# A fused attention and maxout kernel: program order from simulated engines, the score bias added on VectorE, one transpose a step, weights scaled in threes

## The chip, the cores and the metric

The kernel runs on one core of one Trainium2 chip. The metric is the device time in microseconds (us), the median of several executions. The engines are named as in the profile: PE multiplies matrices (PEld is its weight load), DVE and ACT work on vectors, POOL is the slower vector engine, and SP here only issues DMAs. Each engine works through its own instructions strictly in the order in which the program put them; semaphores make one wait for another.

## The reference

```python
# q, k, v: (8, 8, 576, 64); s: (8, 8, 576)
scores = (1 / sqrt(64)) * q @ k.T
cum = cumsum(max(s, 0))
bias = -(cum[:, None] - cum[None, :])
scores = where(causal, -1e9, scores + minimum(bias, 0))
scores = scores - max(scores)
attn = exp(scores); attn = attn / (sum(attn) + 1e-9)
x = (attn @ v)                      # heads side by side: (4608, 512)
h = maximum(maximum(x @ w1, x @ w2), x @ w3)      # (4608, 768)
out = h @ w_out                                   # (4608, 512)
```

Attention is causal, with a decay bias from the running sum of `s`; its rows go through three up projections, of which the largest is kept, and one down projection. Weights come as 64-bit floats.

## The kernel before

**Precision.** Every operand of a matmul is split into a high and a low part, and three products (high x high, high x low, low x high) stand for one.

**Attention.** The 64 heads are taken in 32 pairs (8 batches of 4 pairs). A step is one block of 128 queries of a pair against its causal keys: block `qb` 0 to 3 has 128, 256, 384 or 512 keys for both heads, and block 4 (64 queries, 576 keys) puts both heads on the 128 partitions. There are 160 steps. The first 32 are blocks 0 and 1 of batches 0 to 3, the next 48 are blocks 2 to 4 of the same batches, and the other 80 take batches 4 to 7 whole. A step `t` runs so:

- `scores(t)` on PE: the three products and a fourth one for the bias (`kb` against `qr` or `q4`, prepared from the running sum in `cumulate` and `spread`), and the causal mask through `identb` and `tri`, all added up in a PSUM tile `s`, of which there are two (L329, L333, L349, L353).
- `highest(t)` on DVE: the row maximum `nm` (L360). `expo(t)` on ACT: the exponential in place in PSUM with its sum (L370), then `se` (L374).
- `probs(t)`: the reciprocal `ri` on DVE (L394), the high half `prh` on ACT (L410), and the low half `prl` on DVE, which reads `s` in PSUM and `prh` in SBUF (L413). Then SP issues one DMA transpose of `prh` into `ph` and one of `prl` into `pl` (L416, L422), with a third for the tail of block 4.
- `values` after blocks 1 and 4: the product with the split values `vh` and `vl` into `av` (L463), and the evacuation into the expert input `x` by ACT (L473) and DVE (L474).

The splits of q and k (`prep2`, `prep3`) make `qkh` on ACT and `qkl` on POOL for k (L271) and on DVE for q (L274).

**Weights.** 24 tiles of weights (18 up, 6 down) are decoded from 64 bits by one ACT and three DVE instructions (L495 to L504). They are scaled by a power of two, found in `gram1`, `gram2` and `wscale` for six tiles at once, and split on ACT (L573) and DVE (L578).

**Experts.** 256 or 320 tokens of a batch are a set; there are 16. A set has 18 up groups of 12 matmuls (`pm`, three PSUM tiles, L608) and 4 down groups of 18 (`po`, L650). ACT takes the first `pm` of three to `m` (L622), DVE the maximum with the next two (L625); ACT and POOL split the result into `hh` and `hl` (L614, L615); ACT evacuates `po` (L658).

**Order.** The order is written out in one loop over the steps. Hand-written tables (`begun`, `scaled`, `split`) say at which step which weight is loaded, decoded and split, and a counter `cost` lets expert groups in between the scores according to an assumed PE time of a step (`STEP_NS`).

Of the kernel before, what the change touches and what calls it, by code (L numbers as in the profile page):

```python
# [17 lines left out]
PSUM = bass.MemoryType.PSUM  # L18


@with_exitstack
def kernel(
# [16 lines left out]
    K0 = QP  # L39
# [3 lines left out]
    NFT = NW // 4  # L43
    NB = qkv0.shape[0]
# [33 lines left out]
    R = {}

    def scale_of(v):  # L80
        b, _, qbs = visits[v]
        return (b, 0 if qbs[-1] == 1 else 1)

    def load_start(v, dma):
        g = visits[v][1]
        t = wpool.tile([P, N], F32, tag=f"r{RAW - NP + v}", name=f"st{v}")
        dma(out=t, in_=qkv0[0, g, :, 0:512])
        rv = io.tile([P, QKV - V0], F32, tag=f"rv{g}", name=f"rv{v}")[:, 0:256]
        dma(out=rv, in_=qkv0[0, g, :, 512:768])
        rv = rv.rearrange("p (j k d) -> p j k d", j=2, d=D)  # L90
        R[v] = dict(q=t[:, 0:256], k=t[:, 256:512], rv=rv, c=(0, 512), ko=256, qo=0)

    def load(v, dma=None):
        if v < NP:
            return
        b, g, qbs = visits[v]
        t = io.tile([P, V0], F32, tag="raw", name=f"raw{v}", bufs=2)
        if qbs[-1] == 1:
            (dma or nc.sync.dma_start)(out=t[:, 0:512], in_=qkv0[b, g, :, 0:512])
            R.setdefault(v, {}).update(q=t[:, 0:256], k=t[:, 256:512], c=(0, 512), ko=256, qo=0)  # L100
            return
        c0 = 0 if qbs[0] == 0 else 256
        (dma or nc.sync.dma_start)(out=t[:, c0:V0], in_=qkv[b, g, :, c0:V0])
        R.setdefault(v, {}).update(q=t[:, c0:QP], k=t[:, QP:V0], c=(c0, V0), ko=K0, qo=c0)

    def load_v(v, dma=None):
        if v < NP:
            return
        b, g, qbs = visits[v]
        t = io.tile([P, QKV - V0], F32, tag=f"rv{g}", name=f"rv{v}")  # L110
        src = qkv[b, g, :, V0:QKV]
        if qbs[-1] == 1:
            t, src = t[:, 0:256], qkv0[b, g, :, 512:768]
        (dma or nc.sync.dma_start)(out=t, in_=src)
        R.setdefault(v, {})["rv"] = t.rearrange("p (j k d) -> p j k d", j=2, d=D)

    s_t = att.tile([HB, S], F32, tag="qkh", name="s_t")
    nc.sync.dma_start(out=s_t, in_=s)
    load_start(0, nc.scalar.dma_start)
    load_start(1, nc.sync.dma_start)  # L120
    warm = small.tile([P, 1], F32, tag="warm", name="warm", bufs=1)
    nc.vector.memset(warm, 0.0)
    nc.scalar.activation(out=warm, in_=warm, func=AF.Exp)

    raw_w = {}

    def load_w(i, dma=None):
        w = wpool.tile([P, 2 * N], F32, tag=f"r{i % RAW}", name=f"r{i}")
        (dma or nc.sync.dma_start)(out=w.bitcast(I64), in_=wts[i])
        raw_w[i] = w  # L130


    ident = att.tile([P, P], F32, tag="q4", name="ident")
    make_identity(nc, ident)
    identb = const.tile([P, P], BF16, name="identb")
    tri = const.tile([P, P], BF16, name="tri")
    tri4 = const.tile([P, D], BF16, name="tri4")
    nc.gpsimd.memset(tri, 0.0)
    nc.gpsimd.affine_select(
        out=tri, in_=tri, pattern=[[-1, P]], compare_op=ALU.is_ge, fill=NEG, base=0, channel_multiplier=1  # L140
    )
    nc.gpsimd.memset(tri4, 0.0)
    for j in range(2):
        r = slice(j * D, (j + 1) * D)
        nc.gpsimd.affine_select(
            out=tri4[r], in_=tri4[r], pattern=[[-1, D]], compare_op=ALU.is_ge, fill=NEG, base=0, channel_multiplier=1
        )
    nc.vector.tensor_scalar(out=identb, in0=ident, scalar1=1.0 / VSC, scalar2=None, op0=ALU.mult)
    blk = const.tile([P, P], F32, name="blk")
    nc.gpsimd.memset(blk, 0.0)  # L150
    for j in range(2):
        r = slice(j * D, (j + 1) * D)
        nc.gpsimd.memset(blk[r, r], 1.0)
    ones = const.tile([P, 2], F32, name="ones")
    nc.gpsimd.memset(ones, 0.0)
    sel = io.tile([HB, 2, 2, 160], F32R, tag="raw", name="sel", bufs=2)
    nc.gpsimd.memset(sel.bitcast(F32), 0.0)
    for j in range(2):
        nc.gpsimd.memset(ones[64 * j + 32:64 * j + 64, 0:1], 1.0)
        nc.gpsimd.memset(ones[64 * j:64 * j + 32, 1:2], 1.0)  # L160
        for T in range(2):
            a = 32 * j + 16 * T
            for c in range(2):
                o = 32 + 64 * j + 16 * c
                nc.gpsimd.tensor_copy(out=sel[:, T, c, o:o + 16], in_=ident[0:HB, a:a + 16])
    i16 = const.tile([P, 16], F32, name="i16")
    nc.vector.tensor_reduce(out=i16, in_=ident.rearrange("p (a s) -> p s a", s=16), axis=AX.X, op=ALU.add)


    KB, QR = [], []  # L170

    def cumulate():
        r_t = att.tile([HB, S], F32, tag="qkl", name="r_t")
        nc.vector.tensor_scalar(out=r_t, in0=s_t, scalar1=0.0, scalar2=None, op0=ALU.max)
        c_t = att.tile([HB, S], F32, tag="pTh1", name="c_t", bufs=1)
        nc.vector.tensor_tensor_scan(out=c_t, data0=r_t, data1=r_t, initial=0.0, op0=ALU.add, op1=ALU.max)
        cc = att.tile([HB, 2, S], F32R, tag="pTl1", name="cc", bufs=1)
        nc.vector.tensor_copy(out=cc[:, 0], in_=c_t)
        nc.vector.tensor_tensor(out=cc[:, 1], in0=c_t, in1=cc[:, 0].bitcast(F32), op=ALU.subtract)
        cn = const.tile([HB, 2, 6], F32R, name="cn")  # L180
        cf = cc.bitcast(F32)
        for a, c in ((slice(0, 4), slice(64, Q4, P)), (slice(4, 6), slice(Q4 + 32, Q4 + 34))):
            nc.vector.tensor_scalar(out=cn[:, :, a], in0=cf[:, :, c], scalar1=-1.0, scalar2=None, op0=ALU.mult)
        C.update(cc=cc, cn=cn)

    C = {}

    def spread(T):

        cc, cn = C["cc"], C["cn"]  # L190
        ka = ps_m.tile([P, 512], F32, tag="m", name=f"ka{T}")
        kc = ps_m.tile([P, 512], F32, tag="m", name=f"kc{T}")
        for c in range(2):
            nc.tensor.matmul(ka, lhsT=sel[:, T, c, 32:160], rhs=cc[:, c, 0:512], start=(c == 0), stop=(c == 1))
        for c in range(2):
            nc.tensor.matmul(
                kc[:, 0:64], lhsT=sel[:, T, c, 32:160], rhs=cc[:, c, 512:S], start=(c == 0), stop=(c == 1)
            )
        for c in range(2):
            nc.tensor.matmul(  # L200
                kc[:, 64:70], lhsT=sel[:, T, c, 0:128], rhs=cn[:, c, :], start=False, stop=(c == 1),
                skip_group_check=True,
            )
        kb = const.tile([P, S], F32R, name=f"kb{T}")
        nc.scalar.activation(out=kb[:, 0:512], in_=ka, func=AF.Identity, bias=ones[:, 0:1])
        nc.scalar.activation(out=kb[:, 512:S], in_=kc[:, 0:64], func=AF.Identity, bias=ones[:, 0:1])
        KB.append(kb)
        qr = const.tile([P, 16, 5], F32R, name=f"qr{T}")
        nc.vector.scalar_tensor_tensor(
            out=qr, in0=kc[:, 64:69].unsqueeze(1).to_broadcast([P, 16, 5]), scalar=ones[:, 1:2],  # L210
# [234 lines left out]
    def values(v, ph):  # L445
# [22 lines left out]
        def out():  # L468
# [8 lines left out]
            if g == NP - 1:  # L477
                add_set(b, ph)
# [405 lines left out]
```

## Time and profile before

| | |
|---|---|
| time, median of 3 (lowest, highest) | 995.35 us (994.73, 995.59) |
| the profiled execution | span of 993.9 us, 1.4 us below the median of the times |
| PE busy | 879.7 us (89%), 7580 matmuls |
| DVE busy | 574.7 us (58%) |
| ACT busy | 580.5 us (58%) |
| POOL busy | 171.1 us (17%) |
| DMA | 109.51 MB, mean 110 GB/s |

Busy time is the time in which an engine has an instruction in work; a busy PE can still run at a lower granted clock (1.00 is full speed). In a row of a group the line of the code comes first, then the engine, the operation, output and inputs, the shapes, how often, and behind the bars the busy us and mean ns of one, and the idle us of the engine just before with what ended them. In a row of the timeline the first two numbers are the start and the length in us.

### The profile page before, as it was taken

How to read it: one execution, taken by the hardware profiler on the slowest of the kernel's cores; microseconds unless marked ns; L12 is line 12 of the kernel's file. 1: busy time of each engine (PE TensorE's matmuls, PEld its weight loads, DVE VectorE, ACT ScalarE, POOL GpSimd, SP SyncE). 2: the span in 40 equal slices, each digit the busy share in tenths (PEclk: the TensorE clock that was granted, in tenths of full speed). 3: DMA queues.
4: the chain of work that ended last, by engine and by line, in shares of the span. 5: the costliest groups of instructions: out<-in, count | busy, mean ns of one | idle time of the engine just before them, and what ended most of it. 6: DMA issues, size and time to landing. Idle time of an engine off the chain costs nothing. (4 is left out here: it accounts for less than half of the span.)

```text
span 993.9 us, 20309 instructions
## 1 busy us (share of the span) xinstructions
PE 879.7 (89%) x7580; PEld 664.1 (67%) x7580; DVE 574.7 (58%) x1231; ACT 580.5 (58%) x1574; POOL 171.1 (17%) x235
## 2 busy tenths in 40 slices
PE   3567787799888987998899999999999999998998
PEld 2445565577777755666667677777787767776876
DVE  5777867765656555566465655556565655552211
ACT  4766646765567556566466667565666666562221
POOL 2110221301211212112021121212121111010111
PEclk9977896889999999999999999999999999998999
DMA  7647354346566456574555556554555544533000
GB/s 276 157 99 180 97 144 89 99 110 151 93 133 133 105 132 118 101 161 103 125 100 117 117 99 131 104 122 99 119 89 131 100 100 85 113 64 58 8 22 27
DMA packets 240690, 109.51 MB, mean 110 GB/s; under 512 B 216976, under 2 KB 227216, under 8 KB 240592
## 3 DMA queue, kind: packets, MB, share of 16 engines
q1 hardware_dynamic: 239440, 105.86, 49.5%
q10 hardware_dynamic: 1152, 2.36, 0.8%
q8 instruction: 60, 0.98, 0.4%
q14 instruction: 38, 0.31, 0.1%
HBM read 47.33 MB, written 9.44 MB: 57 GB/s over the span
## 5 line engine op out<-in xcount | busy, mean ns | idle before, releaser
L608 PE MATMUL pm<-x,w 128*128 128x256 f16 (+1 forms) x3456 | 466.8, 292 | 9.5 <-DVE w L578 8.9
L608 PEld LDWEIGHTS <-w 128*128 128x128 f16 x3456 | 336.1, 100 | 99.2 <-DVE w L578 10.8
L413 DVE SCALAR_TENSOR_TENSOR prl<-s,ri,prh 128x384 f16<-128x384 f32 (+3 forms) x288 | 153.0, 568 | 97.3 <-ACT prh L410 62.5
L410 ACT ACTIVATE prh<-s,ri 128x384 f16<-128x384 f32 (+3 forms) x288 | 142.0, 538 | 80.6 <-DVE ri L394 67.9
L615 POOL TENSOR_TENSOR hl<-m,hh 128x256 f16<-128x256 f32 (+1 forms) x96 | 73.0, 761 | 588.1 <-ACT hh L614 549.2
L360 DVE TENSOR_REDUCE nm<-s 128x2 f32<-128x1024 f32 (+4 forms) x160 | 128.2, 801 | 49.1 <-PE s L333 44.9
L370 ACT ACTIVATE s<-s,nm 128x384 f32<-128x384 f32 (+4 forms) x288 | 150.6, 523 | 9.1 <-DVE nm L360 4.9
L625 DVE SCALAR_TENSOR_TENSOR m<-pm,m 128x256 f32<-128x256 f32 (+1 forms) x192 | 87.1, 454 | 114.5 <-PE pm L608 107.4
L650 PE MATMUL po<-hh,w 128*128 128x256 f16 (+1 forms) x768 | 152.2, 290 | 0.0
L650 PEld LDWEIGHTS <-w 128*128 128x128 f16 x1152 | 112.2, 99 | 31.1 <-issue 1.6
L650 PE MATMUL po<-hl,w 128*128 128x320 f16 (+1 forms) x384 | 111.3, 290 | 1.1 <-POOL hl L615 1.1
L614 ACT ACTIVATE hh<-m 128x256 f16<-128x256 f32 (+1 forms) x96 | 42.4, 441 | 116.7 <-DVE m L625 116.5
L329 PE MATMUL s<-qkh 64*128 64x128 f32 (+3 forms) x256 | 57.1, 435 | 46.2 <-DVE prl L413 43.1
L271 POOL TENSOR_TENSOR qkl<-raw,qkh 128x576 fp32r<-128x576 f32 (+1 forms) x44 | 59.8, 1358 | 172.7 <-ACT qkh L264 98.9
L329 PEld LDWEIGHTS s<-qkh 64*128 64x128 f32 x256 | 27.1, 200 | 76.0 <-ACT s L370 52.5
L622 ACT ACTIVATE m<-pm 128x256 f32<-128x256 f32 (+1 forms) x96 | 38.8, 405 | 50.7 <-PE pm L608 50.7
L658 ACT ACTIVATE o<-po,os 128x256 f32<-128x256 f32 (+1 forms) x64 | 32.0, 499 | 62.0 <-PE po L650 56.4
L474 DVE SCALAR_TENSOR_TENSOR x<-av,x 128x256 f16<-128x256 f32 (+1 forms) x64 | 29.1, 454 | 67.5 <-ACT x L473 67.5
L473 ACT ACTIVATE x<-av 128x256 f16<-128x256 f32 (+1 forms) x64 | 26.3, 411 | 65.8 <-PE av L463 65.6
L463 PE MATMUL av<-pl,vh 128*64 128x320 f16 (+3 forms) x384 | 57.4, 285 | 3.9 <-DMA pl<-prl 3.8
L463 PEld LDWEIGHTS <-vh 128*64 128x64 f16 x832 | 45.2, 114 | 20.6 <-issue 15.0
L463 PE MATMUL av<-ph,vh 128*64 128x320 f16 (+3 forms) x384 | 58.2, 292 | 0.0
(108 smaller groups left out, 1039.8 us busy)
## 6 DMA issues: line engine op xcount, KB each, us to landing
r<-in_w_dram SPq DMA_DIRECT2D x22, 512.0 KB, 4.5
rv<-in_qkv_dram SPq DMA_DIRECT2D x32, 320.0 KB, 3.4
raw<-in_qkv_dram SPq DMA_DIRECT2D x16, 608.0 KB, 4.4
raw<-in_qkv_dram SPq DMA_DIRECT2D x16, 480.0 KB, 3.8
out_dram<-o SPq DMA_DIRECT2D x32, 160.0 KB, 2.0
out_dram<-o SPq DMA_DIRECT2D x32, 128.0 KB, 1.9
ph<-prh SPq DMA_TRANSPOSE x192, 2.8
pl<-prl SPq DMA_TRANSPOSE x192, 2.7
```

What stands on the lines that cost most here:

```text
L271: nc.gpsimd.tensor_tensor(out=r["lo"][:, cq:c1], in0=r["k"], in1=r["hi"][:, cq:c1].bitcast(F32), op=ALU.subtract)
L329: nc.tensor.matmul(ps[:, j, :nk], lhsT=lhsT, rhs=rt[rows], start=(n == 0), stop=False, skip_group_check=True)
L360: nc.vector.tensor_reduce(out=nm, in_=sc, axis=AX.X, op=ALU.max, negate=True)
L370: nc.scalar.activation(out=sc, in_=sc, func=AF.Exp, bias=nm[:, j:j + 1], accum_out=sm[:, j:j + 1])
L410: nc.scalar.activation(out=hi, in_=src, func=AF.Copy, scale=sc)
L413: nc.vector.scalar_tensor_tensor(out=lo, in0=src, scalar=sc, in1=hi, op0=ALU.mult, op1=ALU.subtract)
L463: nc.tensor.matmul(av[j * D:(j + 1) * D, c0:nq], lhsT=lt, rhs=rt, start=(n < 2), stop=(n >= len(todo) - 2), skip_group_check=True,)
L608: nc.tensor.matmul(pm[:, :nq], lhsT=w[:, wt, kt, :], rhs=xt, start=(n == 0), stop=(n == 3 * NKT - 1))
L614: nc.scalar.activation(out=st["hh"][:, ft, :nq], in_=m1[:, :nq], func=AF.Copy)
L615: nc.gpsimd.tensor_tensor(out=st["hl"][:, ft, :nq], in0=m1[:, :nq], in1=st["hh"][:, ft, :nq], op=ALU.subtract)
L625: nc.vector.scalar_tensor_tensor(out=m1[:, :nq], in0=pm[:, :nq], scalar=HSC, in1=m1[:, :nq], op0=ALU.mult, op1=ALU.max)
L650: nc.tensor.matmul(pm[:, :nq], lhsT=W[18 + ft][:, wt, dt, :], rhs=st[ht][:, ft, :nq], start=(n == 0), stop=(n == 3 * NFT - 1),)
```

## The change

The kernel is written anew around a planner. Every instruction (or block of matmuls) becomes an `Op` with the engines that may do it, an assumed duration on each, a key and the tiles that it reads and writes. `Plan.run` simulates the five engines once, when the program is built: whenever an engine is free it takes, of the operations that are ready and whose tile is free, the one with the lowest key. The program is then emitted in the order of these starts. Keys let evacuations go first, then attention by step, then expert groups (`1.0e6 + 1000 n`).

```python
 def run(self):
     ...
             for e in engines:
                 if free[e] > now:
                     continue
                 ...
                 op.start, op.eng = now, e
                 op.end = now + dur
                 ...
 def write(self):
     for op in self.seq:
         op.emit(op.eng)
```

What the instructions themselves do differently:

```diff
-                (r["hi"][:, qs], r["lo"][:, ks]),
-                (None, kb[:, :nk]),
...
-        nc.vector.tensor_reduce(out=nm, in_=sc, axis=AX.X, op=ALU.max, negate=True)
+                lambda e, j=j: nc.vector.tensor_tensor_reduce(
+                    out=pj(j), in0=src(j), in1=bias(j), scale=-SCALE, scalar=3.0e38, op0=ALU.add, op1=ALU.min,
+                    accum_out=nm()[:, j:j + 1],
+                ),
...
-                out=sc, in_=sc, func=AF.Exp, bias=nm[:, j:j + 1], accum_out=sm[:, j:j + 1]
+                    out=pj(j), in_=pj(j), func=AF.Exp, scale=-1.0, bias=nm()[:, j:j + 1], accum_out=sm()[:, j:j + 1]
...
-            for c in range(2):
-                nc.sync.dma_start_transpose(
-                    out=pT[c][:, 0:2 * m, i:i + P], in_=halves[c][:, 0:2 * m, :].rearrange("p n c -> p (n c)")
-                )
+                lambda e: nc.sync.dma_start_transpose(
+                    out=pv()[:, 0:4 * m, i:i + P], in_=pr().bitcast(F16)[:, 0:4 * m * P]
+                ),
...
+    chunks = [tuple(range(3 * c, 3 * c + 3)) for c in range(NFT)] + [tuple(range(NUP, NW))]
```

- PE no longer adds the bias. The running sum is written once to DRAM (`cd`), and each pair of heads loads its rows, repeated over the partitions, into `bias` (512 KB) and, for block 4, `b4` (two loads of 144 KB). On DVE one `tensor_tensor_reduce` a head adds it to the scores from PSUM, writes the result to an SBUF tile `p` (two of them) and keeps the row's extreme; in the program it stands as two instructions (L816, shown as ISA).
- The exponential, `pr` high (L861) and `pr` low (L869) then work on `p` in SBUF; the PSUM tile `s` is free once L816 has read it.
- High and low halves of a step lie in one tile `pr` and take one DMA transpose (block 4: two and the tail).
- q is not scaled any more, and `ql` is one POOL instruction over q and k (960 to 1216 columns, L729; for the first loads it may go to DVE). The tile `q4` is gone.
- The scale of the up weights is found for three tiles at a time; the low half of a weight goes to POOL (two instructions) or DVE, wherever the planner finds room: 9 of 24 go to POOL.
- The first evacuation of three (`m`) and that of `x` may go to ACT or DVE: 66 of 96 and 27 of 64 go to DVE.

The first score steps on PE. In the rows before, `kb` against `qr` is the bias and `gmv` a scale of the values:

```order
L329 MATMUL s_192<-qkh_163 128x128 x2
L329 MATMUL s_192<-qkh_163,qkl_166 128x128 x2
L329 MATMUL s_192<-qkl_166,qkh_163 128x128 x2
L329 MATMUL s_192<-kb_187,qr_190 128x128 x2
L333 LDWEIGHTS identb
L333 MATMUL s_192<-tri,identb 128x128
```

And now:

```order
L772 MATMUL s_217<-qh_201 128x128 x2
L772 MATMUL s_217<-qh_201,ql_208 128x128 x2
L772 MATMUL s_217<-ql_208,qh_201 128x128 x2
L776 LDWEIGHTS identb
L776 MATMUL s_217<-tri,identb 128x128
```

The bias pair is gone, and no other row of the step changes.

DVE around step 100, before; `nm` is the maximum, `prl` the split, `m` and `x` are evacuations:

```order
L394 RECIPROCAL ri99_7926<-se99_7907 128x1
L360 TENSOR_REDUCE nm100_7894<-s100_7893 128x2
L413 SCALAR_TENSOR_TENSOR prl99_7929<-s99_7800,ri99_7926,prh99_7928 128x512
L413 SCALAR_TENSOR_TENSOR tl99_7930<-s99_7800,ri99_7926,tl99_7930 128x64
L625 SCALAR_TENSOR_TENSOR m13_1_5_7909<-pm3_1_5_1_7913,m13_1_5_7909 128x320
L625 SCALAR_TENSOR_TENSOR m13_1_5_7909<-pm3_1_5_2_7942,m13_1_5_7909 128x320
L394 RECIPROCAL ri100_7977<-se100_7970 128x2
```

And now, where `p` is the biased score in SBUF and `pr` the split:

```order
L869 SCALAR_TENSOR_TENSOR tl99_7101<-p99_7039,sc_99_7040,tl99_7101 128x64
L816 ISA p100_7121,sc_100_7122<-s100_7012,bias28_6690 128x128
L816 ISA sc_100_7122 128x1
L816 ISA p100_7121,sc_100_7122<-s100_7012,bias28_6690 128x128
L816 ISA sc_100_7122 128x1
L1016 TENSOR_SCALAR m7_2_7141<-u7_2_0_7104 128x320
L869 SCALAR_TENSOR_TENSOR pr99_7125<-p99_7039,sc_99_7040,pr99_7125 128x4x128
```

The reduction has become two pairs of instructions that read PSUM and the bias; the split reads `p` in place of `s`; the first evacuation of `m` (L1016) has come to DVE.

SP at the same place, before:

```order
L416 DMA_TRANSPOSE ph100_7975<-prh100_7979 128x2x128
L416 DMA_TRANSPOSE pl100_7976<-prl100_7980 128x2x128
L659 DMA out_dram<-o3_1_0_8026 128x320
L416 DMA_TRANSPOSE ph100_7975<-prh101_8083 128x4x128
L416 DMA_TRANSPOSE pl100_7976<-prl101_8084 128x4x128
```

And now:

```order
L881 DMA_TRANSPOSE pT0_28_0_7233<-pr100_7210 128x4x128
L881 DMA_TRANSPOSE pT0_28_0_7233<-pr101_7252 128x8x128
L704 DMA bias30_7323<-cd_228 128x2x512
L881 DMA_TRANSPOSE pT1_28_0_7331<-pr102_7294 128x12x128
L714 DMA bl29_7362<-cd_228 64x576 x2
```

A step has one transpose of twice the blocks, and the bias loads stand between them, two units ahead of their use.

Over the whole program the PE order has 39 up groups ahead of step 32 where it had 36, and behind step 159 (the last) it has three up groups and the down groups of set 11 and all of sets 12 to 15, where it had four up groups and the down groups of set 13 and all of sets 14 and 15.

More of the change, by code (lines that the diff above doesn't have):

```diff
@@ L93, in load @@
[L93 to L104, printed above, removed]
@@ L134 @@
[L134 to L140, printed above, removed]
-    )
[L142 to L146, printed above, removed]
-        )
@@ L166 @@
[L166 to L197, printed above, removed]
-            )
[L199 to L202, printed above, removed]
-            )
[L204 to L210, printed above, removed]
-            in1=i16.unsqueeze(2).to_broadcast([P, 16, 5]), op0=ALU.add, op1=ALU.mult,
-        )
-        QR.append(qr)
@@ new lines @@
+    add(
+        {"DVE": (800.0, 720.0)},
+        lambda e: nc.vector.tensor_scalar(
+            out=cct()[0:HB], in0=ct()[0:HB], scalar1=ct()[0:HB, S // 2:S // 2 + 1], scalar2=1.0 / SCALE,
+            op0=ALU.subtract, op1=ALU.mult,
+        ),
+        -1000.0, [ct], [cct],
+    )
+    load(lambda e: E[e].dma_start(out=cd(), in_=cct()[0:HB]), -1000.0, 4 * HB * S, [cct], [cd], queue="ACT")
+    for under in ((st,), (st, rt_), (rt_, ct), (ct, cct), (cct, ident)):
+        seed = Buf(plan, "t", None, "order")
+        for x in under:
+            seed.ops.extend(x.ops)
@@ new lines @@
+    for c in range(len(chunks)):
+        weights(c)
+    units = [("split", b, (2 * h, 2 * h + 1), (0, 1)) for b in range(NB) for h in range(NP // 2)]
+    units += [("rest", b, (g,), (2, 3, 4)) for b in range(NB) for g in range(NP)]
+    units += [("whole", b, (g,), (0, 1, 2, 3, 4)) for b in range(NB, B) for g in range(NP)]
+    begin = []
+    step = 0
+    for kind, b, gs, qbs in units:
+        begin.append(step)
+        step += len(gs) * len(qbs)
+    X, AM, RV, VS = {}, {}, {}, {}
+    nset = [0]
@@ L823 @@
[L823 to L834 removed]
+        n = eset[0]
+        eset[0] += 1
+        if ph:
+            tag = "hb" if count.setdefault("hl", 0) % 2 == 0 else "hc"
+            count["hl"] += 1
+        elif n < NB:
+            tag = ("ha", "hb", "hc", "ha")[n % 4]
+        else:
+            tag = "ha"
@@ L837 @@
+    ahead = 0
+    gone = {"v": 0, "q": 0, "s": 0}
+    for u in range(len(units)):
+        b, kind = units[u][1], units[u][0]
+        while gone["v"] < len(units) and (units[gone["v"]][1], units[gone["v"]][0]) == (b, kind):
+            values_in(gone["v"])
+            gone["v"] += 1
+        qk_in(u)
+        values_split(u)
+        steps(u)
+    plan.run()
+    plan.write()
 _INS = ["q", "k", "v", "s", "moe_w1", "moe_w2", "moe_w3", "moe_w_out"]
```

1445 lines of the change are left out of this document (847 added, 598 removed).

## The prediction

> **What bounds it now.** I read the program in stages: the first score step with three blocks of keys (step 32) starts at 205.23, the last score step (159) ends at 894.6. Columns of the windows: length, then busy us of PE, PEld, DVE, ACT and POOL, granted clock, DMA share, GB/s.
>
> ```profile
> 205.23 0.44 PE L329 MATMUL s<-qkh 64*128 64x384 f32 x2
> ```
> ```profile
> L353 PE MATMUL s<-tri,identb x32: 202/203/277, 201.2 to 894.6; 128*128 128x64 bf16 x32
> ```
> ```profile
> 0.00:205.00 205.00, 136.55 (x1107) 105.64 (x1108) 156.02 (x384) 129.45 (x387) 38.16 (x77) 0.84 0.54 139
> 205.00:525.00 320.00, 287.13 (x2465) 213.88 (x2463) 188.62 (x362) 195.45 (x492) 56.79 (x64) 0.96 0.58 122
> 525.00:900.00 375.00, 368.15 (x3324) 276.69 (x3321) 216.64 (x455) 237.01 (x654) 65.42 (x78) 1.00 0.54 105
> 900.00:994.00 94.00, 87.88 (x692) 67.90 (x689) 13.39 (x30) 18.56 (x43) 10.74 (x17) 0.96 0.08 25
> ```
>
> Up to 205 the busiest engine is DVE (156 of 205, 76%); PE has 137 and a clock of 0.84. From 205 PE is the bound: 655 of 695 us busy to 900, nearly all of it from 525, while DVE has 405 (58%). Next, what PE waits for before 205 (first fence) and from there to 900 (second; columns: us in total, times, longest):
>
> ```profile
> PE s L329 <- DVE prl L413: 39.9, 19, 6.0
> ```
> ```profile
> PE s L349 <- DVE prl L413: 30.7, 17, 3.0
> PE s L329 <- DVE prl L413: 3.2, 4, 1.4
> ```
>
> Scores wait for a PSUM buffer, which is held until the split `prl` of the step two before is done. These are 40 us of the start and 34 us of the middle.
>
> **PE: the bias matmuls go.** Start to start, at a clock of 1.00:
>
> ```profile
> 706.24 0.40 PE L329 MATMUL s<-qkh,qkl 64*128 64x512 f32 x2
> 706.48 0.39 PE L329 MATMUL s<-qkl,qkh 64*128 64x512 f32 x2
> ...
> 711.33 0.28 PE L349 MATMUL s<-qkl,qkh 128*128 128x256 f32 x1
> 711.44 0.28 PE L349 MATMUL s<-kb,q 128*128 128x256 f32 x1
> ...
> 711.86 0.31 PE L349 MATMUL s<-qkl,qkh 128*128 128x320 f32 x1
> 712.00 0.31 PE L349 MATMUL s<-kb,q 128*128 128x320 f32 x1
> ```
> ```profile
> 715.91 0.27 PE L329 MATMUL s<-qkl,qkh 64*128 64x128 f32 x2
> 716.02 0.28 PE L329 MATMUL s<-kb,qr 64*128 64x128 f32 x2
> ...
> 720.71 0.28 PE L329 MATMUL s<-qkl,qkh 64*128 64x256 f32 x2
> 720.84 0.28 PE L329 MATMUL s<-kb,qr 64*128 64x256 f32 x2
> ```
>
> A pair costs 0.11 at 128 keys, 0.13 at 256, 0.24 at 512, so 0.18 at 384, and 0.11 + 0.14 in the tail step: 0.91 for one pair of heads, 29 us over 32 pairs. Of it 16 x (0.18 + 0.24 + 0.25) + 16 x 0.91 = 25 us lie between step 32 and step 159, where PE is the bound; 4 us lie in the start, under DVE. The two preparations of `ka` and `kc` go as well; they lie in the start too.
>
> **PE: order.** Expert matmuls of 256 and 320 columns run at these rates:
>
> ```profile
> 939.75 3.66 PE L608 MATMUL pm<-x,w 128*128 128x256 f16 x32
> 943.24 0.27 PE L650 MATMUL po<-hh,w 128*128 128x256 f16 x1
> ```
> ```profile
> 974.73 6.00 PE L608 MATMUL pm<-x,w 128*128 128x320 f16 x43
> ...
> 980.57 0.30 PE L650 MATMUL po<-hh,w 128*128 128x320 f16 x1
> ```
>
> 3.49/32 = 0.109 and 5.84/43 = 0.136 us. So a set (288 matmuls) is 31.4 or 39.2 us. Behind step 159 the old order has 4 of 18 up groups and all down groups of one wide set (120 matmuls, 16.3), a narrow and a wide set, and the last values: 89 us of work, done in 994 - 895 = 99. The new order has 3 up groups and the down groups of set 11 (14.7), then sets 12 to 15 (two of each kind, 141.2): 158 us. So 69 us of expert work move from the middle to the end, where nothing disturbs PE: the end becomes 168. Before step 32 the new order has 39 up groups and the old 36, another 4 us out of the middle. This moves work and saves none.
>
> Weights in threes add three short chains on DVE; the first up group stands behind step 12 instead of step 13. I give that 0, within 5 us either way, since DVE bounds the start.
>
> **DVE.** First rows of the page, then groups with their shapes (busy us, mean ns):
>
> ```profile
> L413 DVE SCALAR_TENSOR_TENSOR prl<-s,ri,prh 128x384 f16<-128x384 f32 (+3 forms) x288 | 153.0, 568 | 97.3 <-ACT prh L410 62.5
> L615 POOL TENSOR_TENSOR hl<-m,hh 128x256 f16<-128x256 f32 (+1 forms) x96 | 73.0, 761 | 588.1 <-ACT hh L614 549.2
> L360 DVE TENSOR_REDUCE nm<-s 128x2 f32<-128x1024 f32 (+4 forms) x160 | 128.2, 801 | 49.1 <-PE s L333 44.9
> L622 ACT ACTIVATE m<-pm 128x256 f32<-128x256 f32 (+1 forms) x96 | 38.8, 405 | 50.7 <-PE pm L608 50.7
> ...
> r<-in_w_dram SPq DMA_DIRECT2D x22, 512.0 KB, 4.5
> ```
> ```profile
> L413 DVE SCALAR_TENSOR_TENSOR prl<-s,ri,prh 128x512 f16<-128x512 f32 x96 | 69.1, 748 | 43.7 <-ACT prh L410 17.3 <-ACT tl L410 16.7 <-DMA pl<-prl 8.7
> L298 DVE SCALAR_TENSOR_TENSOR vl<-rv,inv,vh 128x640 f16<-128x640 f32 x32 | 28.2, 881 | 0.0
> L394 DVE RECIPROCAL ri<-se 128x2 f32<-128x2 f32 x128 | 20.2, 158 | 33.9 <-ACT se L374 33.6
> L274 DVE SCALAR_TENSOR_TENSOR qkl<-raw,qkh 128x640 fp32r<-128x640 f32 x16 | 17.1, 1070 | 0.0
> L578 DVE SCALAR_TENSOR_TENSOR w<-r,sw,w 128x512 f16<-128x512 f32 x18 | 14.3, 823 | 0.0
> L274 DVE SCALAR_TENSOR_TENSOR qkl<-raw,qkh 128x384 fp32r<-128x384 f32 x16 | 11.0, 685 | 0.0
> L274 DVE SCALAR_TENSOR_TENSOR qkl<-raw,qkh 128x256 fp32r<-128x256 f32 x12 | 5.2, 431 | 0.0
> L578 DVE SCALAR_TENSOR_TENSOR w<-r,rel,w 128x512 f16<-128x512 f32 x6 | 4.2, 743 | 0.0
> ```
>
> The fused bias, minimum and copy is not in the trace. Below: the reduction as it is, 128 us. Above: two input streams at the price of the split (153 us for its 288, and some 9 for the 64 more columns of the tail steps), plus its 288 short second instructions at the reciprocal's 0.158: 207. It is nearest to the split in form; I halve the second part: 185, that is +57. The q split leaves DVE (17.1 + 11.0 + 5.2 and four first ones: -35), 93 evacuations come over from ACT at 0.45 (`L625` below; +42), nine low halves of weights leave for POOL (-7). DVE: 575 + 57 = 632, about 160 of it in the start, 30 at the end, 442 in the middle.
>
> Then comes contention. The split used to read PSUM and one SBUF tile; now it reads two SBUF tiles. The times from least to most:
>
> ```profile
> L274 DVE SCALAR_TENSOR_TENSOR qkl<-raw,qkh x44: 409/554/2021, 42.4 to 868.5; 128x384 fp32r<-128x384 f32 x16, 128x640 fp32r<-128x640 f32 x16, 128x256 fp32r<-128x256 f32 x12
> ```
> ```profile
> L625 DVE SCALAR_TENSOR_TENSOR m<-pm,m x192: 412/452/493, 79.4 to 980.8; 128x256 f32<-128x256 f32 x96, 128x320 f32<-128x320 f32 x96
> ```
> ```profile
> L271 POOL TENSOR_TENSOR qkl<-raw,qkh 128x576 fp32r<-128x576 f32 x32 | 49.1, 1534 | 130.5 <-ACT qkh L264 61.7 <-issue 23.6 <-PE s L333 16.5
> ```
>
> `L625`, with one SBUF input, never stretches; `L274`, with two, reaches 2021, twice its longest form's mean. `L578` shows the usual size: 823 against 743 for one form, 0.08. POOL's instruction grows: 1216 columns where there were 576, so some 2.6 us on average over the forms of the new one (960 to 1216), at 1.53 for 576. The 288 two-tile instructions of the middle lose 23 us at 0.08 each. If each instead meets POOL at random, it loses (31 x 2.6 squared + 70 x 0.8 squared) over twice 574, 0.22 us: 64 in all. I take 45 between them. By the Trainium skill (SBUF — State Buffer, "Who interferes with whom") a VectorE instruction with two SBUF inputs and a GpSimd instruction that reads SBUF lock each other out for the whole instruction, which speaks against this change; the trace agrees.
>
> **ACT, POOL, DMA.** ACT loses the 93 evacuations at 0.4 (`L622`; 580 to about 540), POOL goes from 171 to about 215 (41 larger `ql`, nine weights, no `q4`): neither bounds. Transposes go from 416 issues to 224; values wait for them hardly at all:
>
> ```profile
> PE av L463 <- DMA pl<-prl: 3.8, 3, 1.8
> ```
>
> so that is worth at most 4 us, and the later release of `pr` may take as much: 0. The bias costs 40 loads of 512 KB and 64 of 144 KB, 30 MB on 110; the DMA share goes from 0.55 to some 0.65, loaded five steps ahead where 512 KB of weights land in 4.5, so hidden; a late one would hold DVE, with every evacuation behind it. The path from `s` through DRAM makes the first step some 3 us later, covered by weight decoding.
>
> **Sum.** Start 205: DVE has the same work there (about 160) plus stretch, against the freed PSUM wait; between 180 (wait gone, DVE at 89%) and 220. Middle 689 - 25 - 69 - 4 = 591; of the 34 us of waits I take half as gone: 574, where PE still has the most work and DVE 442 + 45 = 487 (85%). End 168. Span 947; the median shown lies 1.4 above the span of the profiled execution (995.35 against 993.9; what surrounds the span): 948.
>
> **Rivals.**
> - Likeliest, 0.50: as summed, 925 to 975.
> - Gain in full, 0.20: all score waits vanish: start 180, middle 557, end 166: 903 + 1 = 904. For it: scores need only the new instruction two steps back. Against: DVE then must run at 87%.
> - DVE takes over, slower, 0.24: its in-order queue, stretched by POOL, does not exceed the 76% of the start. Middle 487/0.76 = 641: 205 + 641 + 168 + 1 = 1015. It decides for slower below 78% (621 us). Against: until now DVE was never the engine that had to keep up.
> - No gain, 0.03: stalls give back just what the matmuls save: 995.
> - Half-rate split, 0.03: if two SBUF inputs halved the rate, the middle would carry some 80 us more on DVE, 567/0.85 = 667: 1041. Against: `L298` reads two SBUF tiles, 881 at 640, the rate of `L413` from PSUM (748 at 512). The Trainium skill says that it halves (Vector Engine (DVE) Microarchitecture Reference, "Points that are easy to get wrong"); this trace disagrees.
>
> **Numbers.** 948, likeliest case 925 to 975. The range takes in the full gain and most of the DVE case: 900 to 1018, with some 0.1 outside on each side. Faster by over 0.2% (about what can be told here): 0.72; within: 0.04; slower: 0.24.
>
> **What would show it.** Right: no wait of scores on the split; DVE 80% or more busy in the middle, splits stretched to over 1 us; PE over 90% after 205; about 165 us of pure expert matmuls at the end. Wrong: PE idle behind DVE in the middle (late evacuations, `m` buffers), DVE waiting for a bias load, or a start much off 205.

## The result, and the profile after

| | before | after |
|---|---|---|
| median, us (lowest to highest of 4 runs) | 995.47 (994.73 to 996.78) | 905.53 (902.87 to 907.65) |
| ratio to before (95% interval) | | 0.910 (0.9078 to 0.9122) |
| profiled execution: span, us | 993.9 | 901.1 |

The kernel is 90 us faster. The forecast was 948 in a range of 900 to 1018: the sign and the range held, the likeliest case (925 to 975) did not, and the number that came is that of the rival "gain in full" (904). Its mechanism came only in part, as will be seen.

First a correction. The prediction took 205.23 as the start of step 32; that row belongs to step 35. The first score matmul over 384 keys, which is step 32, stands in the timeline of PE, before and after (and then step 35 of after), at:

```profile
189.53 0.44 PE L329 MATMUL s<-qkh 64*128 64x384 f32 x2 [2.79 <-DVE prl L413]
```
```profile
168.41 0.44 PE L772 MATMUL s<-qh 64*128 64x384 f32 x2
...
180.38 0.44 PE L772 MATMUL s<-qh 64*128 64x384 f32 x2
```

With these borders and the end of the last scores (894.6 before, 739.2 after) the windows of before and then of after read as follows (length; busy us of PE, PEld, DVE, ACT, POOL; granted clock; DMA share; GB/s):

```profile
0.00:190.00 190.00, 126.15 (x1042) 98.22 (x1044) 142.99 (x360) 118.25 (x361) 35.61 (x73) 0.87 0.55 143
190.00:895.00 705.00, 660.68 (x5809) 494.49 (x5807) 415.44 (x839) 441.13 (x1168) 124.32 (x145) 0.97 0.55 113
895.00:994.00 99.00, 92.88 (x735) 71.41 (x733) 16.24 (x35) 21.10 (x48) 11.18 (x17) 0.97 0.12 28
```
```profile
0.00:168.00 168.00, 112.21 (x997) 87.39 (x998) 150.28 (x436) 107.64 (x308) 74.48 (x83) 0.98 0.72 195
168.00:739.00 571.00, 545.59 (x4955) 409.28 (x4953) 431.74 (x1154) 403.22 (x1051) 132.69 (x104) 1.00 0.84 180
739.00:901.00 162.00, 158.63 (x1304) 125.04 (x1302) 40.80 (x91) 25.96 (x58) 18.63 (x26) 1.00 0.11 29
```

In stages: start 189.5 to 168.4 (-21), middle 705.1 to 570.8 (-134), end 99.3 to 161.9 (+63). The matmul counts say what the end is: 569 more there, and 854 fewer in the middle. Of those 854, 569 went to the end, 256 are the bias matmuls of 128 steps, and 29 went to the start. So 63 us of the middle are only moved; net it gained 72, the start 21.

Between the prediction's own borders (step 35 and the last scores) start and middle of after read:

```profile
0.00:180.38 180.38, 124.32 (x1107) 97.02 (x1108) 160.91 (x467) 117.57 (x336) 82.46 (x88) 0.98 0.72 194
180.38:739.20 558.82, 533.68 (x4846) 399.75 (x4846) 421.30 (x1123) 393.49 (x1022) 124.70 (x99) 1.00 0.85 180
```

What PE waits for in the middle of after, and over the whole span what ACT waits for before it can write `pr`:

```profile
PE s L772 <- DVE sc L816: 15.5, 23, 1.6
...
PE s L784 <- DVE sc L816: 2.2, 4, 0.8
```
```profile
ACT pr L861 <- DMA pT<-pr: 32.5, 36, 2.7
```

The 34 us of score waits of the middle became 17.7, with L816 as the new releaser. The last row is the wait that the prediction put at nothing ("the later release of `pr`"): ACT waits until a transpose has emptied a `pr` tile. It stays short here, but the experiments on transposes hang on it.

On DVE and POOL, groups by shape where the shape matters (busy us, mean ns), and last the windows of `L816` alone (DVE busy, each moment counted once):

```profile
L869 DVE SCALAR_TENSOR_TENSOR pr<-p,sc,pr 128x384 f16<-128x384 f32 (+3 forms) x288 | 185.0, 669 | 77.7 <-ACT pr L861 76.7
...
L729 POOL TENSOR_TENSOR ql<-qr,qh 128x960 fp32r<-128x960 f32 (+3 forms) x41 | 101.6, 2479 | 158.4 <-ACT qh L722 107.6
...
L816 DVE CUSTOM_DVE_ANT_0 p<-s,bias 128x128 f32<-128x128 f32 (+3 forms) x256 | 117.1, 483 | 6.0 <-DMA bias<-cd 3.4
```
```profile
L869 DVE SCALAR_TENSOR_TENSOR pr<-p,sc,pr 128x512 f16<-128x512 f32 x96 | 85.8, 914 | 34.2 <-ACT pr L861 33.7
...
L816 DVE CUSTOM_DVE_ANT_0 p<-s,bl 128x576 f32<-128x576 f32 x32 | 24.0, 750 | 0.6
L816 DVE DVE_READ_ACCUMULATOR2_ANT sc<- 128x1 f32 x288 | 23.4, 81 | 0.0
```
```profile
0.00:901.10 901.10, 142.41 (x576) 1.00 0.69 155
```

The rows of the fused bias add up to 117.1 + 24.0 + 23.4 = 164.5 us, but its instructions overlap in part: together they keep DVE busy for 142.4 (the prediction took 185). The split has become slower, 914 ns for 512 columns where it took 748 from PSUM, 32 us over its 288.

### The profile page after: what moved, and what is told of

The parts are those of the page before. It is cut to its first block, busy times and chain, and to the rows that moved or that the text cites. A ratio compares the mean times of both kernels' runs of the same rounds, so it can differ in the third digit from the quotient of the medians.

```text
span 901.1 us, 19766 instructions
## 1 busy us (share of the span) xinstructions
PE 816.4 (91%) x7251; PEld 621.7 (69%) x7251; DVE 622.8 (69%) x1679; ACT 536.8 (60%) x1414; POOL 225.8 (25%) x212
## 4 chain that ended last, share of the span: by engine, by line
PE 34%; DVE 8%; ACT 5%; issue 3%; DMA 3%; DVEq 0%; ACTq 0%
PE u L1001 21%; PE d L1055 7%; DVE pr L869 3%; DMA pT<-pr 3%; PE s L772 3%; ACT pr L861 2%; PE av L924 2%; ACT p L825 1%; DVE p L816 1%; PE s L776 1%; DVE m L1024 1%; PE s L784 1%; DVE vv L646 1%; ACT qh L722 0%; ACT vv L641 0%
## 5 line engine op out<-in xcount | busy, mean ns | idle before, releaser
L1001 PE MATMUL u<-x,w 128*128 128x256 f16 (+1 forms) x3456 | 446.3, 287 | 2.7 <-DVE x L957 1.5
L869 DVE SCALAR_TENSOR_TENSOR pr<-p,sc,pr 128x384 f16<-128x384 f32 (+3 forms) x288 | 185.0, 669 | 77.7 <-ACT pr L861 76.7
L825 ACT ACTIVATE p<-p,sc 128x384 f32<-128x384 f32 (+4 forms) x288 | 165.8, 576 | 82.7 <-DVE sc L816 81.7
L861 ACT ACTIVATE pr<-p,sc 128x384 f16<-128x384 f32 (+3 forms) x288 | 152.0, 569 | 55.5 <-DMA pT<-pr 32.5
L1036 POOL TENSOR_TENSOR h<-m,h 128x256 f16<-128x256 f32 (+1 forms) x96 | 76.7, 799 | 382.2 <-ACT h L1031 382.1
L1024 DVE SCALAR_TENSOR_TENSOR m<-u,m 128x256 f32<-128x256 f32 (+1 forms) x192 | 86.9, 452 | 91.5 <-PE u L1001 90.1
L1055 PE MATMUL d<-h,w 128*128 128x256 f16 (+1 forms) x1152 | 147.7, 286 | 0.0
L729 POOL TENSOR_TENSOR ql<-qr,qh 128x960 fp32r<-128x960 f32 (+3 forms) x41 | 101.6, 2479 | 158.4 <-ACT qh L722 107.6
L816 DVE CUSTOM_DVE_ANT_0 p<-s,bias 128x128 f32<-128x128 f32 (+3 forms) x256 | 117.1, 483 | 6.0 <-DMA bias<-cd 3.4
L772 PE MATMUL s<-qh 64*128 64x128 f32 (+3 forms) x256 | 55.4, 425 | 49.4 <-DVE sc L816 40.2
L924 PE MATMUL av<-pT,vv 128*64 128x320 f16 (+3 forms) x1152 | 78.7, 281 | 1.5 <-DMA pT<-pr 1.1
L1016 DVE TENSOR_SCALAR m<-u 128x256 f32<-128x256 f32 (+1 forms) x66 | 29.9, 454 | 41.0 <-PE u L1001 38.1
```

The source lines that it names most:

```text
L729: lambda e, c0=c0, c1=c1: E[e].tensor_tensor(out=lo().bitcast(F32R)[:, c0:c1], in0=raw()[:, c0:c1], in1=hi()[:, c0:c1], op=ALU.subtract),
L772: nc.tensor.matmul(ps[:, j, :nk], lhsT=lt[rs], rhs=rt[rs], start=(n == 0), stop=False, skip_group_check=True)
L816: lambda e, j=j: nc.vector.tensor_tensor_reduce(out=pj(j), in0=src(j), in1=bias(j), scale=-SCALE, scalar=3.0e38, op0=ALU.add, op1=ALU.min, ...
L825: lambda e, j=j: nc.scalar.activation(out=pj(j), in_=pj(j), func=AF.Exp, scale=-1.0, bias=nm()[:, j:j + 1], accum_out=sm()[:, j:j + 1]),
L861: lambda e, h_=h_, s_=s_, j=j: nc.scalar.activation(out=h_(), in_=s_(), func=AF.Copy, scale=ri()[:, j:j + 1]),
L869: lambda e, h_=h_, l_=l_, s_=s_, j=j: nc.vector.scalar_tensor_tensor(out=l_(), in0=s_(), scalar=ri()[:, j:j + 1], in1=h_(), op0=ALU.mult, ...
```

## The experiments

All times are medians, with the 95% interval of the ratio to before (run on the same chip each time). "Same order" says that the planned order of after was kept; the others were planned anew, and that alone can shift a time: an example is below.

### What the bias is worth on PE

`e1_fourth_product` gives PE work of the same width back, in the same order.

```diff
-for n, (lt, rt) in enumerate((..., (h[:, qs], l[:, ks]))):
+for n, (lt, rt) in enumerate((..., (h[:, qs], l[:, ks]), (l[:, qs], l[:, ks]))):
```

> The changed kernel with a fourth product (low x low) added to every score step, in the order planned without it: the same shape and number of matmuls as the bias pair of the kernel before. If PE is the bound from step 32 to step 159 (0.91 us for each pair of heads, 25 us there, nothing in the start), the time goes from 905.5 to about 930. Rival: the order and DVE set the pace of the middle and PE has room, then 905 to 912.

Measured: 911.99 us, ratio 0.9158 (0.9136 to 0.9181), 6.5 us above after. The middle of this kernel, and its waits for scores over the span (40.2 in after):

```profile
168.00:749.00 581.00, 567.72 (x5212) 431.97 (x5210) 432.27 (x1155) 403.56 (x1052) 133.27 (x104) 1.00 0.84 177
```
```profile
PE s L772 <- DVE sc L816: 29.9, 18, 16.4
```

PE has 22 us more to do in the middle, the stage takes 10 us longer: the rest is done in time that PE had waited in. The rival held, at the edge of its range.

`e2_before_no_bias_matmul` takes the bias matmuls out of before (the scores then lack the decay bias).

```diff
-                (None, kb[:, :nk]),
...
-                    (r["q4"], kb[:, k0:k0 + nk]),
```

> The kernel before without the bias matmuls of the score steps (the decay bias is left out of the scores); all else, the preparation of the bias too, as before. If these matmuls lie on the path from step 32 on, 995.5 falls by 25 to 29, to 966 to 970. Rival: the scores' wait for the split of two steps before takes the place of the matmuls, and the time stays above 980. In both cases some 60 us are left to the other parts of the change.

Measured: 980.35 us, ratio 0.9847 (0.9820 to 0.9874): 15 us, not 25 to 29, and at the border of the rival (above 980). Here the waits for a PSUM buffer over the span, in before and then without the bias matmuls:

```profile
PE s L329 <- DVE prl L413: 43.1, 23, 6.0
...
PE s L349 <- DVE prl L413: 33.5, 18, 3.0
```
```profile
PE s L328 <- DVE prl L411: 46.9, 26, 6.2
PE s L347 <- DVE prl L411: 39.5, 20, 3.6
```

They grew by 10. Work taken from PE reaches the time in part only, in either order; the rest comes back as a wait.

### What the early release of PSUM is worth

`e3_p_in_psum` leaves the biased scores in PSUM, so that `s` is held until the split, as before. Planned anew.

```diff
-        pt = buf("p", name=f"p{t}")
+        pt = sp
```

> The changed kernel with the biased scores written back into their PSUM tile instead of the SBUF tile p, replanned: the PSUM tile is held until the split is done, as before, and the split reads one SBUF tile. Theory that the early release of PSUM made the start short (168 us where it was 205) and took the score waits out of the middle: start 190 to 205, middle up by 10 to 30, in all 935 to 965. Rival that the order alone did it, and that the locks between DVE and POOL cost: splits back from 0.91 to 0.75 us at 512, and 895 to 908 in all.

Measured: 917.71 us, ratio 0.9221 (0.9194 to 0.9247), 12 us above after and between the two expectations. The start is 181.7 (after 168.4), with 75 matmuls more in it (1074, after 999); middle and end together are 734.1 (after 732.7), with about as many fewer. The split is a releaser of the scores again, and, with one input from PSUM, it is as short as in before:

```profile
PE s L772 <- DVE pr L870: 21.0, 16, 8.1
```
```profile
L870 DVE SCALAR_TENSOR_TENSOR pr<-s,sc,pr 128x512 f16<-128x512 f32 x96 | 70.0, 747 | 40.5 <-ACT pr L862 29.7 <-ACT tl L862 10.8
```

So the 12 us are a net: the splits take 29 us less of DVE, and `L816`, which now writes to PSUM, takes 24 more (166.5).

### What the plan is worth

`e8_prices_halved` lets the plan believe that DVE and ACT are twice as fast; the instructions are the same.

```diff
                 dur, busy = op.ways[e][:2]
+                if e in ("DVE", "ACT"):
+                    dur, busy = 0.5 * dur, 0.5 * busy
```

> The changed kernel planned with half the duration on DVE and ACT, all else the same: the same instructions in an order made for engines that do not exist. Theory that the plan's right durations keep DVE at 89% in the start: start 185 or more, PE waits behind late DVE work in the middle, in all 925 to 970. Rival that priorities and buffers set the order and durations hardly matter: 900 to 912.

Measured: 1083.26 us, ratio 1.0885 (1.0849 to 1.0922). Its middle, and the two longest waits of ACT:

```profile
201.00:873.00 672.00, 551.57 (x4681) 400.64 (x4678) 458.29 (x1166) 390.51 (x1000) 124.37 (x96) 0.93 0.70 151
```
```profile
ACT p L827 <- DVE sc L818: 250.5, 144, 10.2
...
ACT h L1033 <- DVE m L1026: 181.2, 70, 4.7
```

Neither expectation was near. The same work is 178 us slower than after, and slower than the order written by hand: PE has 552 us of work in 672. A planned order is worth only as much as the durations it was planned with.

### Threes

`e4_weights_in_sixes`, planned anew:

```diff
-    chunks = [tuple(range(3 * c, 3 * c + 3)) for c in range(NFT)] + ...
+    chunks = [tuple(range(6 * c, 6 * c + 6)) for c in range(NUP // 6)] + ...
```

> The changed kernel with the scale of the up weights found for six tiles at a time, as before, replanned. Theory that threes are worth nothing, since DVE bounds the start (150 of 168 us): 900 to 911. Rival that they let the first experts begin early and so keep PE full: start longer by 10 or more, 915 to 930.

Measured: 907.64 us, ratio 0.9139 (0.9113 to 0.9164): 2 us above after, as the theory had it and less than a new plan can shift. The start is 6 us longer (174.1), the middle 2 shorter.

### DVE against POOL

`e5_no_low_part_of_qk` puts a tile of zeros in place of `ql`, so POOL's large instructions are gone (the two cross products of the scores then add nothing). Planned anew. `e6_low_part_in_quarters` cuts each of them into four; same order. The first and then the second edit:

```diff
-        lo = buf("ql", name=f"ql{u}")
+        lo = zl
```
```diff
-                lambda e, c0=c0, c1=c1: E[e].tensor_tensor(
-                    out=lo()...[:, c0:c1], in0=raw()[:, c0:c1], in1=hi()[:, c0:c1], op=ALU.subtract
+                lambda e, c0=c0, c1=c1: [
+                    E[e].tensor_tensor(out=lo()...[:, x:y], in0=raw()[:, x:y], in1=hi()[:, x:y], ...)
+                    for x, y in (the four quarters of c0 to c1)
```

> The changed kernel without POOL's instruction for the low part of q and k (a zero tile stands in its place in the products, so the two cross terms are left out of the scores), replanned. This takes the long SBUF readers off POOL: the split at 512 columns should fall from 0.91 to near 0.75 us, the sum of the splits by 25 to 30. Theory that DVE and PE are coupled in the middle (PE 96%, DVE 76% busy): 890 to 900. Rival that PE hides it: 902 to 908.

> The changed kernel with each of POOL's instructions for the low part of q and k cut into four, in the same order. If a lock holds for one whole instruction, the splits stretch less (mean 0.67 down to some 0.62 over all shapes, the longest much shorter), while POOL works some 16 us longer in all: 898 to 906. If instead the two share bandwidth, the stretch stays and the time with it or above: 905 to 912.

Measured: 881.05 us, ratio 0.8864 (0.8835 to 0.8893), and 891.17 us, ratio 0.8964 (0.8941 to 0.8987). The split of 512 columns without `ql`, and then with quarters, where the quarters themselves follow:

```profile
L864 DVE SCALAR_TENSOR_TENSOR pr<-p,sc,pr 128x512 f16<-128x512 f32 x96 | 71.2, 761 | 32.6 <-ACT pr L856 32.2
```
```profile
L872 DVE SCALAR_TENSOR_TENSOR pr<-p,sc,pr 128x512 f16<-128x512 f32 x96 | 76.3, 815 | 37.3 <-ACT pr L864 37.0
...
L730 POOL TENSOR_TENSOR ql<-qr,qh 128x240 fp32r<-128x240 f32 (+3 forms) x164 | 135.2, 856 | 153.2 <-ACT qh L722 99.1 <-issue 49.8 <-POOL h L1039 2.7
```

Both gained more than expected. 914, 815, 761 ns: what stretches the split is POOL's instruction, and it counts how long that is in one piece; where the split has one input in PSUM (`e3_p_in_psum`, 747), the same instruction of POOL does not stretch it. In quarters POOL needs 135 us where it needed 102, and the kernel is still 14 us faster. This is the Trainium skill's rule that the prediction weighed (SBUF — State Buffer, "Who interferes with whom"), and the trace agrees. The other rule of the Trainium skill, that two SBUF inputs which are not bf16 halve the rate (Vector Engine (DVE) Microarchitecture Reference, "Points that are easy to get wrong"), does not hold here: 761 ns from SBUF stand beside 748 from PSUM.

The kernel in quarters beats both kernels.

### One transpose a step

`e7_two_transposes` cuts each transpose of scores into two of half the blocks; same order, both behind the split.

```diff
-                lambda e: nc.sync.dma_start_transpose(
-                    out=pv()[:, 0:4 * m, i:i + P], in_=pr().bitcast(F16)[:, 0:4 * m * P]
+                lambda e: [
+                    nc.sync.dma_start_transpose(
+                        out=pv()[:, o:o + 2 * m, i:i + P], in_=pr().bitcast(F16)[:, o * P:(o + 2 * m) * P]
+                    )
+                    for o in (0, 2 * m)
```

> The changed kernel with each transpose cut into two of half the blocks, 416 in all as before, in the same order. Theory that the number of transposes is worth at most 5 us (SP is free, values hardly wait): 903 to 911. Rival that the second issue of 1.2 us a step delays the release of pr, for which ACT already waits 32 us: 915 to 930.

Measured: 993.73 us, ratio 1.0003 (0.9979 to 1.0026). The whole gain is gone. Neither theory had this. The waits (after: 32.5 and 1.1):

```profile
ACT pr L861 <- DMA pT<-pr: 129.7, 88, 4.1
...
PE av L930 <- DMA pT<-pr: 20.8, 33, 3.0
```

This could have been the place of the second half, and a plan that knew only of one. So `e9_two_transposes_planned` puts high and low halves into separate blocks of `pr`, gives each its own transpose that waits for its half alone, and plans anew.

```diff
-                t, [pr], [(pT, qb)],
+                    t, [(pr, (c, j)) for j in range(nj)], [(pT, (qb, c))],
```

> The kernel after with high and low halves in separate blocks of pr, so that each half has a transpose of its own that waits only for its half (as in the kernel before, 416 in all); the plan knows of them at the same price each and orders the program anew. Theory (the 88 us of the kernel with cut transposes came because both went out after the split and the plan knew of one): 903 to 925, waits of ACT for pr below 45 us. Rival (SP and its queue cannot carry 416 transposes in this shorter time, wherever they stand): 950 to 1000, waits of ACT or PE on transposes of 80 us and more.

Measured: 977.14 us, ratio 0.982 (0.9784 to 0.9856), 72 us above after. The rival held: ACT's wait for `pr` is here, and PE waits another 29.4 us for `pT`:

```profile
ACT pr L861 <- DMA pT<-pr: 96.6, 66, 3.8
```

SP's own timeline (start, length, instruction) before and then in this kernel:

```profile
506.37 1.24 SPq L416 DMA_TRANSPOSE ph<-prh  x1
507.82 1.24 SPq L416 DMA_TRANSPOSE pl<-prl  x1
509.15 0.53 SPq L103 DMA_DIRECT2D raw<-in_qkv_dram  x1
```
```profile
507.93 2.77 SPq L883 DMA_TRANSPOSE pT<-pr  x2
510.79 0.53 SPq L1075 DMA_DIRECT2D out_dram<-o  x1
511.42 2.48 SPq L893 DMA_TRANSPOSE pT<-pr  x2
```

A transpose holds SP for 1.2 us and more, a load for 0.53. In the old order SP has gaps; in these rows there are hardly any. A row that stands for several issues runs from the first to the last and takes in the gaps between them, so the sums of the middle are made issue by issue; "under way" is the share of the middle in which at least one transpose is between the start of its issue and its landing:

| | SP busy of the middle | transposes | their mean | other issues | under way |
|---|---|---|---|---|---|
| before | 503 of 705 (0.71) | 348 | 1.27 us | 111 | 0.86 |
| after | 445 of 571 (0.78) | 190 | 1.76 us | 194 | 0.90 |
| cut in two, same order | 600 of 663 (0.90) | 347 | 1.43 us | 194 | 0.97 |
| two planned | 607 of 667 (0.91) | 345 | 1.43 us | 198 | 0.98 |
| two planned, loads on ACT | 507 of 665 (0.76) | 347 | 1.40 us | 44 | 0.97 |

With the 83 further issues of after, mostly loads of the bias, two transposes a step keep SP busy for nine tenths of the middle. The last row is `e12_two_transposes_loads_on_act`, which was to test just this by moving loads from SP to ACT:

```diff
-                k - 8.0, 4 * P * (V0 - c0), writes=[raw],
+                k - 8.0, 4 * P * (V0 - c0), writes=[raw], queue="ACT" if u > 3 else "SP",
```

> The kernel with two planned transposes a step, in which ACT instead of SP issues the loads of q and k, the values and the biases from the fifth pair on (some 150 issues of 0.5 us each; the plan knows of it). In the kernel beside it the queue of SP is busy for 643 of the 667 us between step 32 and step 159 (354 transposes 526, 202 other issues 117). Theory (the issues on SP are the bound there, and this is why one transpose a step is worth 70 us): some 75 us of them leave the middle, SP falls to 565, the middle becomes 590 to 625, and the time 905 to 940. Rival (not SP's issues but the landing of the transposes and the two buffers of pr bound it): no more than 10 us gained or lost, 965 to 990, with the same waits of ACT for pr of 90 us and more. If ACT's own queue becomes the bound: slower than 990.

Measured: 1013.41 us, ratio 1.0207 (1.0163 to 1.0251). The number is that of the last expectation, but its reason is not seen: ACT, its 150 issues counted in, is busy for 435 us of the 665 of the middle. (The 643 us of SP in the expectation had been added up from rows with gaps; issue by issue they are 607.) Here are one such row, the middle, and ACT's wait:

```profile
502.18 17.95 SPq L883 DMA_TRANSPOSE pT<-pr  x8
```
```profile
171.00:836.00 665.00, 576.98 (x4949) 421.99 (x4948) 451.82 (x1167) 405.35 (x1046) 136.84 (x114) 0.95 0.77 154
```
```profile
ACT pr L861 <- DMA pT<-pr: 91.8, 43, 6.7
```

The eight issues of the first row take 12.0 of its 17.95 us; the rest is gaps. And the transposes of `L883` with two planned, then with the loads on ACT (least, median and most ns of an issue):

```profile
L883 SPq DMA_TRANSPOSE pT<-pr x256: 1167/1228/5442, 25.9 to 841.2; - x128
```
```profile
L883 SPq DMA_TRANSPOSE pT<-pr x256: 1167/1227/5507, 27.2 to 844.9; - x128
```

So SP did become free, from 0.91 to 0.76, the issues did not become longer, and the middle stayed as long (665 and 667 us), with some 190 matmuls fewer in it. ACT waits for `pr` nearly as long as with two planned, and the landing of these transposes takes 4.0 us in the median where it took 3.6. That speaks against SP's load as the bound, and for the rival: what the three kernels with two transposes share is that one is under way nearly all the time (0.97 to 0.98). That two transposes a step cost 72 to 88 us in this order, with waits of ACT and PE for `pr` and `pT`, is shown. What sets the pace of the landings is not: no run changes the landing or the number of `pr` buffers alone, and the loads, now issued by ACT, may have cost elsewhere what they freed on SP.

### The order alone

`e10_order_alone` has the planned order with four products a score (their price in the plan), the scores held in PSUM, weights in sixes and two transposes. It still adds the bias on DVE and loads it.

```diff
-        cost = (606.0, 673.0, 848.0, 1019.0, 938.0)[qb]
+        cost = (716.0, 803.0, 1028.0, 1259.0, 1188.0)[qb]
```

> Planned order, but what the instructions do as in the kernel before where it can be had: biased scores back in PSUM with the buffer held until the split, four products a score (the fourth is low x low in place of the bias, at the same width, its price in the plan), weights in sixes, two transposes a step, each for its half. Theory (costs found one by one add: 12 for the PSUM buffer, 6 to 16 for the fourth product, 2 for sixes, and what the two transposes cost in the kernel beside this one): that kernel's time plus 20 to 30, so 925 to 955 if the transposes are nearly free. Rival (the order is worth nothing without the lighter instructions): 985 to 1010.

Measured: 985.06 us, ratio 0.9912 (0.9879 to 0.9945): 10 us better than before, and 8 above the kernel with two planned transposes, where 20 to 30 had been expected from the single costs; it is the lower edge of the rival's range. Beside two transposes, PE's extra work and the later release of PSUM cost little. The parts of the change do not add: undone one by one they cost 6, 12, 2 and 72 us, 92 in sum, and together 80. The order, with the loads of the bias on its shoulders and the work shared among the engines as in after (`ql` on POOL, evacuations on DVE), is worth 10.

### The first bias

`e11_first_loads_held_and_quarters`: in after the first bias lands at 24.6 us, and DVE waits for it. Loads not needed yet are held back; quarters as above; planned anew.

```diff
-                k - 6.0, 8 * P * N, writes=[r], begin=max(0.0, 3000.0 * (i - 3)),
+                k - 6.0, 8 * P * N, writes=[r], begin=0.0 if i < 3 else 16000.0 + 3000.0 * (i - 3),
```

> The kernel with ql in quarters, and the loads of the weights from the fourth on, the values, q and k of the third pair on and later biases held in the plan until 16 to 20 us, so that the first bias does not share the DMA engines. Theory (the first bias lands late because of them): it lands by 18 in place of 25, the start is 7 to 10 shorter, time 880 to 886. Rival (weight decoding was the real length of the start, and the held weights come later): 889 to 900.

Measured: 900.54 us, ratio 0.9046 (0.9009 to 0.9083), 9 above the kernel with quarters alone and just past the range of the rival. The first `L816` in after, and here:

```profile
24.63 0.29 DVE L816 CUSTOM_DVE_ANT_0 p<-s,bias 128x128 f32<-128x128 f32 x1 [3.40 <-DMA bias<-cd]
```
```profile
18.00 0.27 DVE L820 CUSTOM_DVE_ANT_0 p<-s,bias 128x128 f32<-128x128 f32 x1
```

The bias came earlier (with quarters alone at 22.0), as meant. The start shrank from 162.0 to 160.4 only (at a granted clock of 0.84 where it was 0.99), and the middle grew from 566.6 to 578.9 with the same work. An earlier first bias brought the start next to nothing, and this kernel shows what a new plan can shift: some 10 us. By that measure the 2 us of the threes are nothing, and the 12 us of the PSUM buffer are no more than such a shift; what speaks for them is that the split is a releaser again.

## Why the prediction was right or wrong, point by point

- **Borders.** Wrong: step 32 starts at 189.5, not 205. With the right border the same terms give start 189.5, middle 590, end 168, and much the same total (949). Against the measured stages that is 21, 19 and 6 us too much: these are the 46 us between 949 and the profiled 902.87. Between the prediction's own borders it is 205, 574 and 168 against 180.4, 558.8 and 161.9.
- **Start, "same work, 180 to 220", taken as unchanged.** This step failed: the sum kept 205 where its own lower bound, 180 ("wait gone, DVE at 89%"), came almost to the letter. DVE has 160.9 us of work in 180.4, which is 89%, and "about 160" had been said. The waits of scores in the start went from 35.4 to 24.7 us up to step 32, and 16.2 of these are one wait, which ended once the first bias had landed. Holding PSUM longer made the start 13 us longer, though with 75 matmuls more in it and in a new plan.
- **Middle, PE's work.** Moved expert matmuls: 69 predicted, 63 more in the end. Bias matmuls: 25 by counting, but 10 of the stage when put back and 15 of the kernel when taken out of before. A term was missing, and it is most of the 19 us: PE's busy time fell by 115 us where the terms give 98 (25 + 69 + 4). Of the 115, the 598 moved matmuls (62.6 in the end, some 3 in the start) and the bias (25) explain 91. The rest would fit the granted clock, 0.97 to 1.00 over 661 us, an estimate of 20 us. No run took the clock alone.
- **Middle, score waits.** I took half of 34 us as gone: 17.7 remained. Right.
- **End.** 168 predicted, 161.9 measured, PE at 98%. Right in kind.
- **DVE.** 185 for the new instruction was 142; contention of 45 us was 32 on the score splits, and the cause is the one given. These two account for the 54 us by which DVE's total (623) stayed below the forecast (632 + 45). So DVE stood at 432 of 571 (76%), not 85%. The rival "DVE takes over" needed DVE to fall below 78% of a load of 487; between the same borders the load was 421. "Half-rate split" fell with the 761 ns.
- **"Gain in full" (904).** Its total came, and between the prediction's borders its stages too: 180, 557 and 166 against 180.4, 558.8 and 161.9. For the start the mechanism holds. For the middle it doesn't: half of the waits stayed, and the missing term in PE's work made up for them. That part of the hit is luck.
- **Transposes: "worth at most 4 us, 0".** The step that was furthest off. I priced the removed issues by what PE waited for them in the old order. In the new one, where a step lasts 4.5 us in place of 5.5 and loads come on top, a second transpose costs 72 to 88 us. It didn't enter the sum, since the change has one; but the 948 would have stood unchanged for a kernel with two.
- **Bias through DRAM, "3 us later, covered".** DVE starts on the first scores at 24.6 where it was 13.5: 11 us later, and PE waits 16.2 us for it. The other loads land in time, though the DMA share of the middle is 0.84, not 0.65. The run with an earlier first bias gives no sign that this costs the start more than a little.
- **Its signs.** No wait of scores on the split, splits of over 1 us (up to 2.8), PE over 90% and 162 us of experts at the end came. DVE at 80% or more in the middle did not, and "a start much off 205", named as a sign of being wrong, did come.

## What to carry to other kernels

Do not price a removed instruction by what is waited for it now: at 5.5 us a step PE waited 3.8 us for transposes, and in an order of 4.5 us a step, with further loads, a second one costs 72 to 88 us. Add up every in-order queue, the one that only issues DMAs too, issue by issue, and then take load off it in a run: here SP went from 0.91 to 0.76 and nothing was gained. A planned order is as good as its durations, and two plans of nearly the same work can lie 10 us apart; keep the order fixed where a single instruction is to be measured.

## What the runs showed of the hardware

- One issue of a DMA transpose holds SP for 1.23 us in the median where it has half the blocks of a step (two planned) and 1.42 where it has all (`L881` of after), at least 1.17 and at most 5.5; a plain load some 0.53.
- The granted clock does not follow PE's mean busy share alone. Middles that were 0.87 busy had 0.97 (cut in two) and 0.95 (loads on ACT), 0.94 had 0.97 (before), 0.96 had 1.00 (after); but of two starts that were 0.66 and 0.67 busy the first had 0.87 (before), the second 0.98 (after). The Trainium skill says that activity releases the throttle (TensorE: Matmul & The Clock Gate, Part 1); the middles agree in the main, and the starts show that the mean share does not decide it.
- The fused addition and minimum is two instructions on DVE, the second of 81 ns; the first at 576 columns took 750 ns, about as much as the plain reduction from PSUM that it replaced (743). The second overlaps the first in part.
- Cutting a POOL instruction into four cost POOL a third more time and made DVE's instruction with two SBUF inputs 99 ns shorter at 512 columns.
